# A decode step of two layers on one core: 256-key scores on four row bands for the kept heads, and a reordered group before the turn of the layers

## The chip, the cores and the metric

The kernel runs on one core of one Trainium2 chip. The time is device microseconds of one execution. The kernel before was timed three times: 513.09, 513.82 and 517.1 us, median 513.82. One further execution was profiled; its own time was 513.58 us, and the span from its first to its last instruction 511.7 us. All times of views below are microseconds from the start of that span.

## The reference

One token (S = 1, D = 640) goes through two rounds of the same pair of blocks, with the same weights and the same cache in both rounds:

```python
def _A_ref(x, k_cache, v_cache, wq, wo):
    ...
    W = min(4096, max(256, Sk // 4))
    ...
    q = (lambda x, *d: x.transpose(*d))((x @ wq).reshape(B, Sq, Hq, Dh), 0, 2, 1, 3)
    k = jnp.repeat(k_cache[:, :, Sk - W:, :], rep, axis=1)
    v = jnp.repeat(v_cache[:, :, Sk - W:, :], rep, axis=1)
    scores = jnp.einsum("bhqd,bhkd->bhqk", q, k) * (Dh ** -0.5)
    p = _softmax(scores, axis=-1)
    o = jnp.einsum("bhqk,bhkd->bhqd", p, v)
    return (lambda x, *d: x.transpose(*d))(o, 0, 2, 1, 3).reshape(B, Sq, Hq * Dh) @ wo
...
x = A_x
x = x + _A_ref(_layernorm(x, axis=-1), A_k_cache, A_v_cache, A_wq, A_wo)
x = x + _B_ref(_layernorm(x, axis=-1), B_w1, B_w2, B_w3, B_w4)
x = x + _A_ref(_layernorm(x, axis=-1), A_k_cache, A_v_cache, A_wq, A_wo)
x = x + _B_ref(_layernorm(x, axis=-1), B_w1, B_w2, B_w3, B_w4)
return x
```

There are 32 heads with Dh = 192, each with its own K and V, of which the last W = 4096 keys count. K and V of one head are 1536 KB each in bf16. `_B_ref` is a small MLP; with S = 1 its shifted first half is zero, so only w3 and w4 are used. Almost all of the work is reading: K, V, wq, wo, w3 and w4, some 214 MB.

## The kernel before

**Tiling.** A head's 4096 keys lie on 128 partitions, 32 keys in a partition. DVE turns K in place in blocks of 32x32 words (`transpose_half`, L441, two instructions a head). The scores are products with a small block of q as the weights (16 columns: four heads times four row groups) and 512 columns of turned K as the moving operand: six weight blocks times two halves of the keys, 12 products a head (L526). The two halves write different row bands of one PSUM bank, 16 rows at row 0 and 16 at row 32 of a half of the bank; the four heads of a group add up in the same rows. So the scores of a group stand on 64 partitions with 512 keys each, and the next group uses the other 64 partitions.

**Softmax.** `softmax_steps` gives seven steps: `part_max` (DVE reduction of the 64x512 scores, L552), `turn_max` (PE turns the 64 maxima into a row, pmT_ps, L557), `full_max` (DVE, L562 and L565), `spread_max` (PE copies the row back into a column nb_ps, L573; ACT takes it over, L576, and makes the exponentials, L579), `turn_p` (DVE, L585 and L587), `swap` (PE, L599, then ACT L602 and the sums l_ps, L607) and `recip` (L614, L616). Their scratch words lie in o_sb.

**Products with V.** `pv` makes 16 products a head (L649), each with two columns of PT as the weights and 384 columns of V, in four row bands of one bank, O_ps. DVE turns the result into o_sb (L656), and `o_fold` (L663, L664) reduces it. `pv` can be given a function `mid` that is called after the first eight of its 16 products.

**Order.** Heads come in eight groups of four. The first layer goes from heads 28 to 31 down to 0 to 3, the second from heads 0 to 3 up. While a group's products with V run, K of the next group is turned and its scores are made. Within an engine the instructions run in the order in which the program writes them. The group before the last (`hurry` in `attention`) makes the next group's softmax as well, so that the last group starts with its PT.

**Loads.** All loads go through SP's queue in one fixed order (`layer_stream`), into twelve cells of 1536 KB; SP waits until the cell of a load is free, and until the eighth load before it has landed. Everything behind a waiting load waits too. K of heads 0 to 7 stays in its cells, turned, from the first layer to the second (NKEEP = 8), and so do a V and a wo cell; in the second layer a kept head's cell comes free when its scores are made (`give` in `S`). At the turn of the layers few cells are left for the stream. wx_sb holds the rest of w3 and w4 that doesn't fit a cell; it is loaded once, at the end of the first layer (L221, L239, L240).

**V_bank.** Four PSUM banks hold the words of one head's V (VP) from the first layer to the second (`v_words`, L638); O_2 is a part of it that the second layer's first group already uses as a second bank for products with V.

Of the kernel before, what the change touches and what calls it, by code (L numbers as in the profile page):

```python
# [18 lines left out]
P = 128  # L19
# [40 lines left out]
def kernel(  # L60
# [454 lines left out]

    def scores(h, K, ST, hq):

        ng = NGK // NT
        Q = [Qblk[:, h // QH % 2, QAT[hq] + n * QSTEP:][:, 0:QW] for n in range(NCOL)]
        T = K.rearrange("p (j g f i t) -> p g j f i t", j=NJ4, g=NGK, f=NFB, t=2)  # L520
        for f in range(NFB):
            for t in range(2):
                n = 2 * f + t
                for i in range(NT):
                    r = ST[0] + 32 * i
                    nc.tensor.matmul(  # L526
                        ST_both[r:r + QW, :].rearrange("p (g j i) -> p g j i", g=ng, j=NJ4), lhsT=Q[n],
                        rhs=T[:, ng * i:ng * (i + 1), :, f, :, t],
                        start=(hq == 0 and n == 0), stop=(hq == QH - 1 and n == NCOL - 1))

# [2 lines left out]
    nc.vector.memset(ST_both[:], 0.0)  # L533
    turn = [0]

    def next_scores():
        turn[0] += 1
        i = turn[0] % 2 * HP
        return i, ST_both[i:i + HP, :]

    def softmax_steps(n, ST, sc, space, bank=None):

        held = {}
        halves = space.bitcast(BF16)
        at, ST_ps = ST
        S, T = slice(at, at + HP), slice(HP - at, P - at)

        def part_max():  # L550
            pm = short("pm")
            nc.vector.tensor_reduce(out=pm[S, :], in_=ST_ps, op=ALU.max, axis=AX.X)  # L552
            held["pm"] = pm

        def turn_max():
            pmT_ps = psm.tile([1, HP], F32, tag="psm")
            nc.tensor.transpose(pmT_ps[0:1, :], held["pm"][S, 0:1], ident[S, S])  # L557
            held["pmT"] = pmT_ps

        def full_max():  # L560
            ngm = space[0:1, 256:256 + 2 * QH]
            nc.vector.tensor_reduce(out=ngm[:], in_=held["pmT"][0:1, :].rearrange("o (q x m) -> o x q m", q=NT, m=NM),  # L562
                                    op=ALU.max, axis=AX.XY, negate=True)
            wide = space[0:1, 306:306 + HP]
            nc.vector.tensor_scalar(  # L565
                out=wide.rearrange("o (q x m) -> o q x m", q=NT, m=NM),
                in0=ngm[:].unsqueeze(1).unsqueeze(3).broadcast_to([1, NT, 2 * QH, NM]),
                scalar1=sc[0:1, 0:1], scalar2=None, op0=ALU.mult)
            held["w"] = wide

        def spread_max():
            nb_ps = psm.tile([P, 1], F32, tag="psm")
            nc.tensor.matmul(nb_ps[S, :], lhsT=held["w"],  # L573
                             rhs=one[0:1, :], start=True, stop=True)
            nb_sb = space[S, 289:290]
            nc.scalar.copy(nb_sb[:], nb_ps[S, :])  # L576
            Pr = halves[S, 0:SW]
            lpart = space[S, 288:289]
            nc.scalar.activation(out=Pr, in_=ST_ps, func=ACTF.Exp,  # L579
                                 bias=nb_sb[:, 0:1], scale=sc[S, 0:1], accum_out=lpart[:, 0:1])  # L580
            held["Pr"], held["l"] = Pr, lpart

        def turn_p():
            held["PrT"] = halves[T, 0:SW]
            nc.vector.transpose(held["PrT"], held["Pr"])  # L585
            lh = space[S, 280:284]
            nc.vector.tensor_scalar(out=lh[:], in0=hm[S, :], scalar1=held["l"][:, 0:1], scalar2=None, op0=ALU.mult)  # L587
            held["lh"] = lh

        def swap():  # L590
            ng = NGK // NT
            if bank is None:
                PT_ps = psm.tile([P, n, NJ4, NGK], F32, tag="psm")
            else:
                PT_ps = bank[:, 0:n * NJ4 * NGK].rearrange("p (h j g) -> p h j g", j=NJ4, g=NGK)
            src = held["PrT"].rearrange("p (g j i) -> p i j g", g=ng, j=NJ4)
            for m in range(NM):
                for q in range(NT):
                    nc.tensor.matmul(PT_ps[32 * m:32 * (m + 1), :, :, ng * q:ng * (q + 1)], lhsT=Eq[T, (HP - at) // 32 + q, :],  # L599
                                     rhs=src[:, m:QW:NM], start=True, stop=True)  # L600
# [24 lines left out]
    O_ps = O_bank[:, 0:2 * Dh]  # L625
    V_bank = psV.tile([P, 2048], F32, name="V_ps")
    O_2 = V_bank[:, 1024:1024 + 2 * Dh]
    h_ps = V_bank[:, VW:VW + NF // 2], O_bank[:, 2 * Dh:2 * Dh + NF // 2]

    def v_words(layer):  # L630
# [90 lines left out]
    def attention(layer, x_cur, rs_cur, x_new, z_new, rs_new, ss_new):  # L721
# [56 lines left out]
        for step in qa[1:]:  # L778
            step()
        qb[1]()  # L780
        ST = next_scores()
        q1 = qproj_steps(groups[1][0] // QH, xc)
        for hq, h in enumerate(groups[0]):
            for half in range(2):
# [30 lines left out]
        for gi, cur in enumerate(groups):  # L815
# [6 lines left out]
            if nxt:  # L822
                part_max, turn_max, full_max, spread_max, turn_p, swap, recip = softmax_steps(
                    len(cur), ST, sc, o_words, V_bank if layer == 1 and gi > 0 else None)
                ST_n = next_scores()
                if layer == 1 and gi == 0:

                    keep = [hh for hh in nxt if hh[1] < NKEEP]
# [23 lines left out]
                else:  # L852
# [7 lines left out]
                    turn_max()  # L860
                    full_max()
                    spread_max()
                    S(h0, 1, ST_n, 0)
                    h1 = nxt[1][1]
                    q = None
                    if gi + 2 < len(groups):
# [4 lines left out]
                    if layer == 1:  # L871
                        turn_p()
                        PT = swap()
                    if pending is not None:
                        y_ps = out_row(layer, *pending, acc, gi - 1 == rows[0]) if in_row else out_proj(layer, pending)
                    if layer == 0:
# [27 lines left out]
            for hq, h in order:  # L904
# [9 lines left out]
                if layer == 1 and gi == 0:  # L914
                    pv(layer, h, hq, PT, fold, O_2 if h == order[1][1] or h == order[3][1] else O_ps)
                    if early_k:
                        early_t(early_k)

                    def fold(h=h):
                        o_fold(h, oT, rl)  # L920

                    continue
                pv(layer, h, hq, PT, steps[3] if quick and hq == 3 else fold)
                if final:
                    if hq == 0:
# [11 lines left out]
                if quick and hq == 1:  # L937
                    S(h2, 0, ST_n, q2)
                    S(h2, 1, ST_n, q2)
                    T(h3, 0)  # L940
                elif quick and hq == 2:
                    S(h3, 0, ST_n, q3)
                    o_fold(h, oT, rl)
                    S(h3, 1, ST_n, q3)
                    steps = softmax_steps(len(cur), ST_n, sc, kl[:].bitcast(F32), V_bank)
                    for step in steps[:3]:
                        step()
                    continue
                elif hurry and hq == 1:
                    (q2, h2), (q3, h3) = nxt  # L950
                    for half in range(2):
                        T(h2, half)
                        S(h2, half, ST_n, q2)
                    T(h3, 0)
                    S(h3, 0, ST_n, q3)
                    T(h3, 1)
                elif hurry and hq == 2:
                    S(h3, 1, ST_n, q3)
                    steps = softmax_steps(len(cur), ST_n, sc, o_words)
                    steps[0]()  # L960
                    steps[1]()
                elif nxt and not (hurry and hq == 3):
                    q2, h2 = nxt.pop(0)
                    for half in range(2):
                        T(h2, half)
                        S(h2, half, ST_n, q2)
                o_fold(h, oT, rl, len(groups) - 4 > gi >= 2 * layer)
                if hurry and hq == 3:
                    for step in steps[4 if quick else 2:5]:
                        step()  # L970
                    early = steps[5](), steps[6]()
            if final or layer == 1 and gi == 0:
                fold()
# [152 lines left out]
```

## Time and profile before

| | us |
|---|---|
| three timed runs | 513.09, 513.82, 517.1 |
| profiled execution, its own time | 513.58 |
| its span, first to last instruction | 511.7 |
| mean granted TensorE clock over the span | 0.722 |

| group in the profile | count | mean ns of one |
|---|---|---|
| L441 DVE, half of a head's K turned | 112 | 1759 |
| L526 PE, scores, 512 columns | 768 | 507 |
| L649 PE, products with V, 384 columns, O_ps | 968 | 405 |
| L656 DVE, result turned | 62 | 565 |
| L552 DVE, reduction of the scores, 64x512 | 16 | 674 |
| L579 ACT, exponentials, 64x512 | 15 | 773 |
| L585 DVE, turn of P, 64x512 | 15 | 706 |

The mean of a product is its whole passage through a pipeline; several are under way at a time, so the time of a group of products is read from the timeline, not from count times mean. The queue's loads are read from SP's rows in the timeline (when a load is issued) and from the DMA share in a table of stretches (how full the 16 DMA engines are). The share is made from packets, and can stand a few hundredths above 1. The granted clock is the share of full speed that PE was given.

### The profile page before, as it was taken

The numbers are of one execution on the slowest core, as the hardware profiler recorded it, in microseconds if no ns is written. First come the engines' busy times: TensorE is split into PE (matmuls) and PEld (weight loads), VectorE is DVE, ScalarE is ACT, GpSimd is POOL, SyncE is SP. The second block draws the span as 40 slices with busy tenths as digits, with TensorE's granted clock in tenths as the row PEclk, the third lists the DMA queues.
The fourth block names the chain that finished last, engine by engine and source line by source line (L and its number), as shares of the span: only waits on it lengthen the run. The fifth ranks groups of instructions, "written<-read, shape, count | busy, mean of one in ns | idle before, by whom it ended". The sixth has DMA issues, their size and how long they took to land. (4 is left out here: it accounts for less than half of the span.)

```text
span 511.7 us, 7558 instructions
## 1 busy us (share of the span) xinstructions
PE 293.1 (57%) x3188; PEld 141.8 (28%) x3188; DVE 297.4 (58%) x492; ACT 52.1 (10%) x173; POOL 3.7 (1%) x16
## 2 busy tenths in 40 slices
PE   1145747546275463855665885848474762726585
PEld 0011313213132231422232432414231331312254
DVE  2086686557574584567633236776777475656622
ACT  1000101010010101001010111011110101001101
POOL 2000000000000000000000000000000000000000
PEclk9995685858767686585665597775869596787855
DMA  8999999999999999999999999999999999999995
GB/s 369 430 430 428 430 444 430 439 430 412 454 432 409 438 420 424 432 417 453 428 376 413 369 422 428 437 430 439 427 416 439 438 425 430 417 433 432 423 409 215
DMA packets 12005, 214.50 MB, mean 419 GB/s; under 512 B 2564, under 2 KB 3076, under 8 KB 7428
## 3 DMA queue, kind: packets, MB, share of 16 engines
q1 hardware_dynamic: 11972, 214.02, 98.2%
q8 instruction: 25, 0.41, 0.3%
q14 instruction: 8, 0.07, 0.0%
HBM read 214.01 MB, written 0.00 MB: 418 GB/s over the span
## 5 line engine op out<-in xcount | busy, mean ns | idle before, releaser
L441 DVE STREAM_TRANSPOSE cell<-cell 128x1536 uint32<-128x1536 uint32 x112 | 194.6, 1759 | 35.5 <-DMA cell<-in_A_k_cache_dram 34.9
L526 PE MATMUL ST_ps<-cell,Qblk 128*16 128x512 bf16 x768 | 151.1, 507 | 71.4 <-DVE cell L441 53.8
L649 PE MATMUL O_ps<-cell,PT 128*2 128x384 bf16 x968 | 90.3, 405 | 8.3 <-DMA cell<-in_A_v_cache_dram 7.6
L526 PEld LDWEIGHTS <-Qblk 128*16 128x16 bf16 x768 | 45.3, 105 | 145.0 <-issue 123.4
L656 DVE STREAM_TRANSPOSE o_sb<-O_ps 128x384 f32<-128x384 f32 x62 | 35.0, 565 | 45.3 <-PE O_ps L649 45.3
L649 PEld LDWEIGHTS <-PT 128*2 128x2 bf16 x1024 | 36.7, 90 | 29.4 <-issue 21.5
L486 DVE TENSOR_TENSOR o_sb<-qT_ps,words 128x24 bf16<-128x24 f32 (+1 forms) x18 | 3.2, 179 | 51.1 <-PE qT_ps L482 28.9
L557 PE MATMUL pmT_ps<-ident,words 64*1 64x64 f32 x16 | 4.0, 252 | 48.7 <-DVE words L552 48.7
L585 DVE STREAM_TRANSPOSE o_sb<-o_sb 64x512 bf16<-64x512 bf16 x15 | 10.6, 706 | 24.6 <-ACT o_sb L579 24.6
L664 ACT ACTIVATE words<-oT_ps,words 32x6 bf16<-32x6 f32 x40 | 10.3, 257 | 143.0 <-PE oT_ps L663 83.1
L663 PE MATMUL oT_ps<-o_sb,Lq 128*32 128x6 f32 x160 | 12.5, 186 | 11.8 <-DVE o_sb L656 11.3
L573 PE MATMUL nb_ps<-words,o_sb 1*64 1x1 f32 x30 | 4.9, 230 | 24.8 <-DVE o_sb L565 24.8
L663 PEld LDWEIGHTS oT_ps<-o_sb,Lq 128*32 128x32 f32 x160 | 10.9, 128 | 22.4 <-issue 15.6
L461 PE MATMUL qr_ps<-wq_sb,words 128*1 128x384 bf16 x90 | 15.8, 514 | 0.0
L557 PEld LDWEIGHTS pmT_ps<-ident,words 64*1 64x1 f32 x16 | 1.2, 76 | 51.7 <-issue 51.7
L669 ACT ACTIVATE words<-oT_ps,words 32x6 bf16<-32x6 f32 x24 | 6.2, 257 | 92.1 <-PE ST_ps L526 64.3
L472 PE MATMUL qT_ps<-words,wq_sb 128*128 128x1 bf16 x210 | 7.2, 165 | 13.0 <-DMA wq_sb<-in_A_wq_dram 12.2
L552 DVE TENSOR_REDUCE words<-ST_ps 64x1 f32<-64x512 f32 x16 | 10.8, 674 | 5.0 <-PE ST_ps L526 4.9
L695 PE MATMUL yr_ps<-cell,words 128*1 128x320 bf16 x108 | 13.4, 406 | 0.0
L576 ACT COPY o_sb<-nb_ps 64x1 f32<-64x1 f32 x15 | 2.3, 153 | 95.3 <-PE nb_ps L573 95.3
L573 PEld LDWEIGHTS nb_ps<-words,o_sb 1*64 1x64 f32 x30 | 4.0, 189 | 27.8 <-issue 26.2
L579 ACT ACTIVATE o_sb<-ST_ps,o_sb,words 64x512 bf16<-64x512 f32 x15 | 11.6, 773 | 0.5
(161 smaller groups left out, 202.7 us busy)
## 6 DMA issues: line engine op xcount, KB each, us to landing
cell<-in_A_k_cache_dram SPq DMA_DIRECT2D x56, 1536.0 KB, 27.7
cell<-in_A_v_cache_dram SPq DMA_DIRECT2D x56, 1536.0 KB, 27.7
cell<-in_A_wo_dram SPq DMA_DIRECT2D x13, 960.0 KB, 27.7
wq_sb<-in_A_wq_dram SPq DMA_DIRECT2D x5, 1536.0 KB, 13.5
cell<-in_A_v_cache_dram SPq DMA_DIRECT2D x6, 768.0 KB, 23.7
cell<-in_B_w_dram SPq DMA_DIRECT2D x1, 1536.0 KB, 12.6
cell<-in_B_w_dram SPq DMA_DIRECT2D x2, 768.0 KB, 10.3
cell<-in_A_wo_dram SPq DMA_DIRECT2D x3, 480.0 KB, 17.0
```

The source lines that it names most:

```text
L441: nc.vector.transpose(Ku, Ku)
L461: nc.tensor.matmul(qr_ps[32 * i:32 * i + 1, :], lhsT=xc[:, kc:kc + 1], rhs=wq_sb[:, kc, t0 * P + i * N:t0 * P + (i + 1) * N], start=(kc == ...
L526: nc.tensor.matmul(ST_both[r:r + QW, :].rearrange("p (g j i) -> p g j i", g=ng, j=NJ4), lhsT=Q[n], rhs=T[:, ng * i:ng * (i + 1), :, f, :, ...
L552: nc.vector.tensor_reduce(out=pm[S, :], in_=ST_ps, op=ALU.max, axis=AX.X)
L573: nc.tensor.matmul(nb_ps[S, :], lhsT=held["w"], rhs=one[0:1, :], start=True, stop=True)
L579: nc.scalar.activation(out=Pr, in_=ST_ps, func=ACTF.Exp, bias=nb_sb[:, 0:1], scale=sc[S, 0:1], accum_out=lpart[:, 0:1])
L585: nc.vector.transpose(held["PrT"], held["Pr"])
L649: nc.tensor.matmul(O_ps[r:r + 2, :], lhsT=PT[:, hq, 2 * i:2 * i + 2], rhs=v_pair(V, h, 2 * i * Dh, 2 * Dh), start=(i < 4), stop=(i >= NB - 4))
L656: nc.vector.transpose(o_sb[:], O_ps.rearrange("p (e a c) -> p e c a", e=2, c=NA))
L663: nc.tensor.matmul(oT_ps[r, :], lhsT=Lq[:], rhs=o_sb[:, e, :, e], start=(e == 0), stop=(e == 1))
L664: nc.scalar.activation(oT[r, :], oT_ps[r, :], ACTF.Copy, scale=rl[r, 0:1])
L695: nc.tensor.matmul(yr_ps[32 * i:32 * i + 1, :], lhsT=oT[:, k:k + 1], rhs=wo_t[:, k * D + i * N:k * D + (i + 1) * N], start=(k == 0), stop= ...
```

## The change

Four things are changed.

1. In the second layer the scores of groups 0 and 1 (heads 0 to 7, those whose K was kept) stand on 128 partitions with 256 keys each. `next_scores` takes the number of bands (`nt`, 4 or 2); with 4 it gives one half of the bank's columns on all partitions. `scores` then makes 24 products of 256 columns a head in four row bands, in place of 12 of 512 in two. The softmax of these two groups works on 128x256, and its `swap` has 16 products in place of 8.
2. In the second layer's group 1 the scores of the next group's first head (head 8, which is loaded) are made behind `swap`, in place of ahead of the q products (`late`).
3. In the first layer's group before the last (heads 4 to 7) a new block takes the place of the `hurry` branches. Heads 5 and 7 write O_2, heads 4 and 6 O_ps. Head 5's products follow head 4's at once, then come head 1's scores, and K of heads 2 and 3 is turned in one run. The softmax of the last group gets its words in wx_sb (`wx_sb[:, 0:6 * P]`) in place of o_sb; `turn_max` is issued ahead of head 7's products, `full_max` and `spread_max` in the middle of them.
4. O_2 is cleared at the start (one DVE memset of 128x384).

The program's instructions on each engine follow this: on PE 12 weight loads and 12 products more for each of the eight kept heads, and 8 of each more for the two swaps; one memset more on DVE, the same loads in the same order on SP. Some waits change with it: the load of the w3 rest into wx_sb waits for DVE and ACT.

```diff
     def scores(h, K, ST, hq):
 
-        ng = NGK // NT
+        at, ST_ps, nt = ST
+        ng = NGK // nt
...
-                for i in range(NT):
-                    r = ST[0] + 32 * i
+                for i in range(nt):
+                    r = 32 * i
                     nc.tensor.matmul(
-                        ST_both[r:r + QW, :].rearrange("p (g j i) -> p g j i", g=ng, j=NJ4), lhsT=Q[n],
+                        ST_ps[r:r + QW, :].rearrange("p (g j i) -> p g j i", g=ng, j=NJ4), lhsT=Q[n],
...
-    def next_scores():
+    def next_scores(nt=NT):
+
         turn[0] += 1
-        i = turn[0] % 2 * HP
-        return i, ST_both[i:i + HP, :]
+        if nt == NT:
+            i = turn[0] % 2 * HP
+            return i, ST_both[i:i + HP, :], nt
+        i = turn[0] % 2 * SW // 2
+        return 0, ST_both[:, i:i + SW // 2], nt
...
-        at, ST_ps = ST
-        S, T = slice(at, at + HP), slice(HP - at, P - at)
+        at, ST_ps, nt = ST
+        np_, w = 32 * nt, 2 * SW // nt
+        S = slice(at, at + np_)
+        T, t_at = (slice(HP - at, P - at), (HP - at) // 32) if nt == NT else (S, 0)
...
-            held["PrT"] = halves[T, 0:SW]
+            held["PrT"] = halves[T, 0:w] if nt == NT else halves[T, w:2 * w]
...
     O_2 = V_bank[:, 1024:1024 + 2 * Dh]
+    nc.vector.memset(O_2, 0.0)
...
-        ST = next_scores()
+        ST = next_scores(4 if layer == 1 else NT)
...
-                ST_n = next_scores()
+                ST_n = next_scores(4 if layer == 1 and gi == 0 else NT)
...
-                    S(h0, 1, ST_n, 0)
+                    late = layer == 1 and gi == 1
+                    if not late:
+                        S(h0, 1, ST_n, 0)
...
                     if layer == 1:
                         turn_p()
                         PT = swap()
+                    if late:
+                        S(h0, 1, ST_n, 0)
...
+                if hurry and layer == 0:
+                    if hq == 1:
+                        mid = fold
+                    elif hq == 3:
+                        steps[1]()
+                        mid = steps_23
+                    else:
+                        mid = None
+                    pv(layer, h, hq, PT, mid, O_2 if hq % 2 else O_ps)
+
+                    def fold(h=h):
+                        o_fold(h, oT, rl)
+
+                    if hq == 0:
+                        continue
+                    if hq == 1:
+                        h1 = nxt.pop(0)[1]
+                        S(h1, 1, ST_n, 1)
+                        fold()
+                        (q2, h2), (q3, h3) = nxt
+                        for hh in (h2, h3):
+                            T(hh, 0)
+                            T(hh, 1)
+                        S(h2, 1, ST_n, q2)
+                    elif hq == 2:
+                        S(h3, 1, ST_n, q3)
+                        fold()
+                        steps = softmax_steps(len(cur), ST_n, sc, wx_sb[:, 0:6 * P].bitcast(F32))
+                        steps[0]()
+
+                        def steps_23():
+                            steps[2]()
+                            steps[3]()
+                    else:
+                        fold()
+                        steps[4]()
+                        early = steps[5](), steps[6]()
+                    continue
...
-                elif hurry and hq == 1:
-                    (q2, h2), (q3, h3) = nxt
-                    for half in range(2):
-                        T(h2, half)
-                        S(h2, half, ST_n, q2)
-                    T(h3, 0)
-                    S(h3, 0, ST_n, q3)
-                    T(h3, 1)
-                elif hurry and hq == 2:
-                    S(h3, 1, ST_n, q3)
-                    steps = softmax_steps(len(cur), ST_n, sc, o_words)
-                    steps[0]()
-                    steps[1]()
...
                 if hurry and hq == 3:
-                    for step in steps[4 if quick else 2:5]:
-                        step()
+                    steps[4]()
                     early = steps[5](), steps[6]()
```

More of the change, by code (lines that the diff above doesn't have):

```diff
@@ L555, in turn_max @@
         def turn_max():
-            pmT_ps = psm.tile([1, HP], F32, tag="psm")
+            pmT_ps = psm.tile([1, np_], F32, tag="psm")
             nc.tensor.transpose(pmT_ps[0:1, :], held["pm"][S, 0:1], ident[S, S])
@@ L561, in full_max @@
             ngm = space[0:1, 256:256 + 2 * QH]
-            nc.vector.tensor_reduce(out=ngm[:], in_=held["pmT"][0:1, :].rearrange("o (q x m) -> o x q m", q=NT, m=NM),
+            nc.vector.tensor_reduce(out=ngm[:], in_=held["pmT"][0:1, :].rearrange("o (q x m) -> o x q m", q=nt, m=NM),
                                     op=ALU.max, axis=AX.XY, negate=True)
-            wide = space[0:1, 306:306 + HP]
+            wide = space[0:1, 306:306 + HP] if nt == NT else space[0:1, w // 2:w // 2 + np_]
             nc.vector.tensor_scalar(
-                out=wide.rearrange("o (q x m) -> o q x m", q=NT, m=NM),
-                in0=ngm[:].unsqueeze(1).unsqueeze(3).broadcast_to([1, NT, 2 * QH, NM]),
+                out=wide.rearrange("o (q x m) -> o q x m", q=nt, m=NM),
+                in0=ngm[:].unsqueeze(1).unsqueeze(3).broadcast_to([1, nt, 2 * QH, NM]),
                 scalar1=sc[0:1, 0:1], scalar2=None, op0=ALU.mult)
@@ L576, in spread_max @@
             nc.scalar.copy(nb_sb[:], nb_ps[S, :])
-            Pr = halves[S, 0:SW]
+            Pr = halves[S, 0:w]
             lpart = space[S, 288:289]
@@ L590, in swap @@
         def swap():
-            ng = NGK // NT
+            ng = NGK // nt
             if bank is None:
@@ L597, in swap @@
             for m in range(NM):
-                for q in range(NT):
-                    nc.tensor.matmul(PT_ps[32 * m:32 * (m + 1), :, :, ng * q:ng * (q + 1)], lhsT=Eq[T, (HP - at) // 32 + q, :],
+                for q in range(nt):
+                    nc.tensor.matmul(PT_ps[32 * m:32 * (m + 1), :, :, ng * q:ng * (q + 1)], lhsT=Eq[T, t_at + q, :],
                                      rhs=src[:, m:QW:NM], start=True, stop=True)
```

## The prediction, made before the changed kernel ran

> **What bounds the kernel now.** I read the page's busy times and DMA queue first, then a table of stretches for the DMA share, then the chain of waits, and last the timeline where the DMA share falls.
>
> ```profile
> PE 293.1 (57%) x3188; PEld 141.8 (28%) x3188; DVE 297.4 (58%) x492; ACT 52.1 (10%) x173; POOL 3.7 (1%) x16
> q1 hardware_dynamic: 11972, 214.02, 98.2%
> ```
>
> No engine passes 58% of the span, while the load queue's packets fill 98.2% of the 16 DMA engines' time. The stretches say where the rest is (columns: stretch, its length, busy time of PE, PEld, DVE, ACT and POOL, granted clock, DMA share, GB/s):
>
> ```profile
> 2.60:264.00 261.40, 139.77 (x1310) 63.65 (x1314) 157.01 (x230) 22.90 (x74) 0.96 (x4) 0.73 1.00 431
> 264.00:267.00 3.00, 3.00 (x62) 1.77 (x58) 0.92 (x4) 0.26 (x1) 0.00 (x0) 0.50 0.77 261
> 267.00:291.00 24.00, 14.84 (x254) 9.37 (x245) 8.35 (x39) 3.03 (x14) 0.00 (x0) 0.50 1.01 404
> 291.00:295.00 4.00, 4.00 (x35) 1.47 (x32) 0.43 (x3) 0.47 (x2) 0.00 (x0) 0.89 0.76 284
> 295.00:503.90 208.90, 128.10 (x1459) 62.74 (x1457) 128.59 (x201) 23.03 (x76) 0.71 (x2) 0.74 1.00 427
> 503.90:511.70 7.80, 3.10 (x90) 2.66 (x87) 2.07 (x14) 1.16 (x5) 0.00 (x0) 0.50 0.24 92
> ```
>
> From 2.6 to 503.9 us the DMA share is 1.00 or 1.01 but for two dips. Gap A (264 to 267) is 3.00 x 0.23 = 0.69 us of missing transfer, gap B (291 to 295) 4.00 x 0.24 = 0.96; together 1.65 us. That sum is what this change can win, since it touches neither the bytes, nor the start, nor the 7.8 us behind the last loads. The chain of waits agrees: its long pieces from 346.6 us on are loads, down to the last.
>
> ```profile
> 470.90 23.66 DMA cell<-in_A_v_cache_dram
> 494.57 10.29 DMA cell<-in_B_w_dram
> ```
>
> Both gaps begin because SP's next load waits for a cell that PE still reads.
>
> **Part 1: products in two banks, own words for softmax (gap A).** The group is heads 4 to 7 of the first layer, next to last in order. Before:
>
> ```profile
> 258.17 0.81 PE L649 MATMUL O_ps<-cell,PT 128*2 128x384 bf16 x13
> 260.06 0.21 DVE L562 TENSOR_REDUCE o_sb<-pmT_ps 1x8 f32<-1x64 f32 x1 [0.45 <-PE oT_ps L663]
> 260.69 0.24 PE L573 MATMUL nb_ps<-words,o_sb 1*64 1x1 f32 x2 [0.68 <-DVE o_sb L565]
> 263.70 1.45 PE L649 MATMUL O_ps<-cell,PT 128*2 128x384 bf16 x16
> 265.20 2.05 SPq L182 DMA_DIRECT2D cell<-in_A_v_cache_dram  x4
> ```
>
> The turned maxima are in pmT_ps at 258.09, but the full maximum starts at 260.06: its result goes into o_sb, which head 7's fold still reads. With its words in wx_sb it needs only pmT_ps. In the second layer the same pair is 0.30 apart (transpose 316.77, reduction 317.07), so the reduction starts at 257.88 + 0.30 = 258.2 and nb_ps, 0.63 later as before (260.06 to 260.69), is ready to run at 258.8. PE runs eight of head 7's sixteen products ahead of it (258.1 to 258.5) and eight behind. Eight cost 0.4 to 0.7 us (half of a group of 16, 0.82 at clock 1.0, 1.45 at 0.5): with nb_ps's 0.24 between them V_ps is complete by 259.8, and turned by DVE (0.58) by 260.4. The 0.70 turn of P (L585), behind it on DVE, ends at 261.1; from there to the first products it is 263.70 - 262.82 = 0.88. Head 0's products start at 262.0 in place of 263.70 and end at 263.45; SP issues at 263.5 in place of 265.20, 1.7 us earlier. Before, the share was whole again 1.3 us after that issue (266.5); now that is 264.8, where it first fell at 264.5 (in half microseconds the shares from 264.5 are 0.15, 0.58, 0.57, 0.67). Some 0.2 of 0.69 is left: gain 0.5.
>
> Head 5's products move ahead of head 1's scores, which frees head 5's cell about 1.2 us earlier (a load issued at 245.47); transfers are whole there, so nothing. K of heads 2 and 3 is turned in the same DVE places; head 6's products wait for their V (from 252.3 to 253.0), so everything up to 257.0 stays. The load at 259.02 comes at about 259.8, 0.8 later. Cover: SP issued nothing more until 265.20, yet the share held until 264.5; less that load's own 960 KB (2.3 us at 431 GB/s) and 1.3 of start, 1.9 us. The w3 rest that goes into wx_sb (issued at 268.18) now also waits for the softmax words there, free by 262.5: cover 5.7 us. The new memset of V_ps lies in DVE's idle start (its neighbour of 128x512 took 0.48): nothing.
>
> From 266.4 to 291 the work waits for loads (V at 270.73 and 276.68, w4 at 284.49 by the releasers), so the 0.5 passes on to gap B.
>
> **Part 2: 256 keys on 128 partitions (gap B).**
>
> ```profile
> 288.75 2.73 PE L526 MATMUL ST_ps<-cell,Qblk 128*16 128x512 bf16 x12 [0.27 <-DVE Qblk L510]
> 291.51 0.33 SPq L157 DMA_DIRECT2D cell<-in_A_k_cache_dram  x1
> 307.83 0.82 PE L649 MATMUL O_ps<-cell,PT 128*2 128x384 bf16 x16
> ```
>
> Head 0's twelve products end at 291.48; SP issues at 291.51 into an emptying queue. They become 24 of 256 columns in four bands: 24 x 256 / 4 = 1536 columns a band, where the twelve stream 12 x 512 / 2 = 3072. The P times V products also use four bands: 16 x 384 / 4 = 1536. So I take their time, 1.45 us at clock 0.50 and 0.82 at 1.00, for 2.73 and 1.53 now. Lower end 0.82 (full clock), upper end 24 x 2.73 / 12 = 5.46 (a product costs as much as today, however short); I take 1.45, since that row has the same columns, bands and engine, and the clock was 0.50 here. So head 0 starts at 288.75 - 0.5 and ends at 289.7; SP issues at 289.75, 1.76 earlier than before, while the data ahead of it end 0.5 earlier: 1.26 won against them. The next load, behind head 1's scores, left at 293.22; now it is 289.8 + 1.45, about 291.3, 1.4 won likewise. The dip lasted from 291.5 (0.92 in the half microsecond before, then 0.41, 0.67, 0.48) to about 294.5, a third of the transfers short on average. Its first half, 291.5 to 293.0, is the waiting for the first load (0.72 of the 0.96), and a start 1.26 earlier takes nearly all of it; of the rest, while the queue fills again, I keep all: gain 0.7.
>
> The Trainium skill speaks against this part: "TensorE: Matmul & The Clock Gate", section "Back-to-back issue gap", gives about 81 ns per product at 128 columns and 131 at 512 in a stream of weight loads and products. An estimate between them, 98 ns at 256, makes 24 products 2.35 us. The trace has 1.53 / 12 = 128 ns for 512 columns, which fits, but 0.82 / 16 = 51 ns for 384 in four bands, which doesn't.
>
> The other seven kept heads shorten by 0.6 to 1.3 us each, and so do the two softmaxes: reduction 0.69, exponential 0.77 and turn 0.70 handle half the columns. The swap has 16 products for 8 (0.44 before; at most 0.88). All of this is under a DMA share of 1.00: nothing.
>
> Moving head 8's scores behind the swap adds about 1.4 us to the cell whose K load left at 321.95; queued behind it on PE are out_proj's products and head 4's, and on SP every later load. Cover: from 291.51 to 315.13 nine loads of 1536 KB, one of 960 and one of 384 were issued, 15.5 MB, 36 us at 431 GB/s, so the queue lasts to about 328.5. That leaves 6.6 us, less 1.3 of start and the 1.2 won: nothing.
>
> **Sum.** 0.5 + 0.7 = 1.2 us. The profiled execution took 513.58 us (span 511.7 and 1.9 around it), so 512.4; the median of the three runs, 513.82, is 0.24 above it. I keep 512.4.
>
> **Rivals.**
> - A floor per weight load and product: twice as many of half the length, and head 0's scores stay at 2.73, B with them. Only A's 0.5 is won: 513.1. By the Trainium skill's estimate above, 2.35, it would be 0.4 less. For: twice the products and weight loads (PEld's mean for them is 105 ns). Against: 51 ns in four bands. Chance 0.12.
> - The gaps close but a later dip takes it back: cells come free at PE's pace between 295 and 346, and a queue that is 1.2 us ahead finds its cell taken. Then 513.6. For: SP's issues wait for PE until 346.64. Against: the reserve above. Chance 0.13.
> - Slower: products in four bands of 16 rows, not 2, cost as much each as those of 512. Head 0 takes 5.46, ends at 293.7, and SP issues 2.2 us later than before: 513.58 + 2.2 = 515.8, A's gain being eaten in the same wait. It decides from 24 x 135 ns = 3.23, where B's loss equals A's 0.5. Against: the columns above. Chance 0.07.
> - Forecast, 1.2 of 1.65 won: 0.62. The rest, 0.06, is what I don't see.
>
> **Numbers.** A measurement here tells some 1% (5.1 us) from no change. The whole missing transfer between start and tail is 1.65 us, so faster by more than that has 0.02; slower, a queue stall that I don't see, 0.05; same 0.93. Low end: the fastest run, 513.09, less 1.65 = 511.4. High end: the median without a gain, 513.8, and half a microsecond of the runs' spread: 514.4. The slower rival lies outside.
>
> **What would show it.** In the changed profile: DMA share near 1 around 264 to 267 and 290 to 294; the four V loads out near 263.6; score groups of 24 at 128x256 near 1.45 us at clock 0.5 and 0.8 at 1.0; the first K load of head 8 near 289.8; no new dip up to 346. Scores over 2.7 us, or a dip near 325, would make the prediction wrong.

## The result, and the profile after

| kernel | set of runs | runs | median us | lowest to highest |
|---|---|---|---|---|
| before | first | 8 | 513.85 | 512.78 to 517.10 |
| changed | first | 8 | 511.79 | 511.58 to 512.13 |
| before | third | 27 | 513.01 | 511.73 to 516.07 |
| changed | third | 12 | 512.20 | 511.41 to 513.52 |

The ratio of changed to before is 0.9952, with a 95% interval of 0.9934 to 0.9971, in the first set of runs, and 0.9981 (0.9968 to 0.9995) when it was measured again in the third (the second holds experiments 1 to 4). So the change makes the kernel faster by something between 0.05% and 0.7%, which is less than the 1% that the prediction took for the least that a measurement can tell. The forecast of 512.4 us is 0.6 above the first median. As a gain it was 1.2 us; the runs side by side give 2.1 in one set and 0.8 in the other, and 0.9952 times 513.82, the median that the prediction had of the kernel before, is 511.35, just below its low end of 511.4.

The profiled execution of the changed kernel took 512.13 us, its span 510.3 (before: 513.58 and 511.7). Busy times and the load queue from its page:

```profile
span 510.3 us, 7783 instructions
PE 290.5 (57%) x3300; PEld 144.4 (28%) x3300; DVE 297.1 (58%) x493; ACT 51.8 (10%) x173; POOL 3.7 (1%) x16
q8 instruction: 26, 0.43, 0.3%
```

PE has 112 products more and is 2.6 us less busy; DVE, which has the largest share, is nearly unchanged (297.1 for 297.4). The table of stretches, with the columns of the prediction (length, busy time of PE, PEld, DVE, ACT, POOL, clock, DMA share, GB/s), cut finer behind gap A:

```profile
2.60:264.00 261.40, 140.16 (x1352) 65.09 (x1353) 158.63 (x235) 23.11 (x75) 0.96 (x4) 0.75 1.00 431
264.00:267.00 3.00, 0.84 (x12) 0.37 (x15) 0.00 (x0) 0.10 (x1) 0.00 (x0) 0.50 0.85 357
267.00:281.00 14.00, 8.18 (x119) 4.80 (x112) 5.45 (x18) 1.40 (x7) 0.00 (x0) 0.50 1.01 412
281.00:284.00 3.00, 1.22 (x46) 1.14 (x44) 1.82 (x13) 1.33 (x6) 0.00 (x0) 0.50 0.95 334
284.00:290.00 6.00, 5.21 (x125) 4.05 (x126) 1.23 (x11) 0.30 (x2) 0.00 (x0) 0.50 1.02 404
290.00:295.00 5.00, 4.49 (x101) 3.00 (x90) 0.81 (x5) 0.46 (x2) 0.00 (x0) 0.75 0.95 333
295.00:502.40 207.40, 126.95 (x1477) 63.11 (x1477) 127.06 (x198) 22.66 (x76) 0.71 (x2) 0.71 1.00 429
```

In the DMA share, gap A (264 to 267) rose from 0.77 to 0.85 and gap B, taken from 290 to 295, from 0.80 to 0.95. Between them is a dip that the kernel before did not have: 281 to 284 moves 334 GB/s, where it moved 416. The two stretches of before:

```profile
281.00:284.00 3.00, 1.78 (x61) 1.70 (x61) 1.63 (x15) 1.06 (x4) 0.00 (x0) 0.50 1.11 416
290.00:295.00 5.00, 5.00 (x39) 1.73 (x36) 0.43 (x3) 0.47 (x2) 0.00 (x0) 0.82 0.80 310
```

The timeline shows what starts the loads at the three places (start, duration, engine, line, operation, operands, count, idle time and its releaser). At gap A, products in two banks, with the other words and the turned maxima between them:

```profile
256.04 0.21 PE L564 MATMUL pmT_ps<-ident,words 64*1 64x64 f32 x1 [0.87 <-DVE words L559]
256.29 0.21 DVE L569 TENSOR_REDUCE wx_sb<-pmT_ps 1x8 f32<-1x64 f32 x1 [0.40 <-PE pmT_ps L564]
256.61 0.50 PE L657 MATMUL V_ps<-cell,PT 128*2 128x384 bf16 x8 [0.36 <-DMA cell<-in_A_v_cache_dram]
257.04 0.27 PE L580 MATMUL nb_ps<-words,wx_sb 1*64 1x1 f32 x2
257.24 0.50 PE L657 MATMUL V_ps<-cell,PT 128*2 128x384 bf16 x8
260.25 1.45 PE L657 MATMUL O_ps<-cell,PT 128*2 128x384 bf16 x16
261.74 2.58 SPq L182 DMA_DIRECT2D cell<-in_A_v_cache_dram  x4
```

The full maximum (L569) starts 0.25 us behind the turn into pmT_ps, where before it waited until 260.06 for head 7's fold; SP issues the four V loads at 261.74 in place of 265.20. Part of this is the granted clock, which was 1.00 here from 250 to 258 and 0.50 to 0.54 in the profile of before; experiment 5 has the comparison at half clock. At the new dip, the last w3 products on a cell and the load that takes the cell, in the changed kernel and then in the kernel before:

```profile
280.82 0.78 PE L1059 MATMUL O_ps<-words,cell 128*128 128x1 bf16 x24
281.63 3.79 SPq L157 DMA_DIRECT2D cell<-in_A_v_cache_dram  x2
```

```profile
281.68 0.78 PE L1023 MATMUL O_ps<-words,cell 128*128 128x1 bf16 x24
282.49 3.72 SPq L157 DMA_DIRECT2D cell<-in_A_v_cache_dram  x2
```

SP issues 0.03 us behind those products in both, so it waits for PE there too. Why the queue runs empty only in the changed kernel is seen in the landings. A load is split over the 16 DMA engines and lands with 16 completions, one for each engine's part. On average over four profiled executions of each kernel, this V load leaves 0.6 us earlier (281.84 for 282.45). The load ahead of it, the last of w4, is complete on its first engine 1.8 us earlier (282.12 for 283.90), and on its last 0.6 us earlier. So the first engine is out of work 0.3 us after the V load is issued, where it was 1.45 us. And at gap B, the first two heads of layer 2:

```profile
287.94 1.46 PE L527 MATMUL ST_ps<-cell,Qblk 128*16 128x256 bf16 x24 [0.28 <-DVE Qblk L510]
289.45 0.33 SPq L157 DMA_DIRECT2D cell<-in_A_k_cache_dram  x1
289.46 1.46 PE L527 MATMUL ST_ps<-cell,Qblk 128*16 128x256 bf16 x24
290.96 0.33 SPq L182 DMA_DIRECT2D cell<-in_A_v_cache_dram  x1
```

Twenty-four products of 256 columns take 1.46 us, where twelve of 512 took 2.73.

### The profile page after: what moved, and what is told of

Same layout as the page of the kernel before. It is cut to its first block, busy times and chain, and to the rows that moved or that the text cites. A ratio compares the mean times of both kernels' runs of the same rounds, so it can differ in the third digit from the quotient of the medians.

```text
span 510.3 us, 7783 instructions
## 1 busy us (share of the span) xinstructions
PE 290.5 (57%) x3300; PEld 144.4 (28%) x3300; DVE 297.1 (58%) x493; ACT 51.8 (10%) x173; POOL 3.7 (1%) x16
## 5 line engine op out<-in xcount | busy, mean ns | idle before, releaser
L527 PE MATMUL ST_ps<-cell,Qblk 128*16 128x512 bf16 (+1 forms) x864 | 147.5, 478 | 72.0 <-DVE cell L441 56.0
L664 DVE STREAM_TRANSPOSE o_sb<-O_ps 128x384 f32<-128x384 f32 x60 | 33.8, 563 | 48.3 <-PE O_ps L657 48.3
L657 PEld LDWEIGHTS <-PT 128*2 128x2 bf16 x1024 | 38.0, 91 | 34.7 <-issue 25.4
L564 PE MATMUL pmT_ps<-ident,words 64*1 64x64 f32 (+1 forms) x16 | 4.2, 263 | 45.7 <-DVE words L559 45.7
L592 DVE STREAM_TRANSPOSE o_sb<-o_sb 64x512 bf16<-64x512 bf16 (+1 forms) x14 | 9.4, 668 | 22.3 <-ACT o_sb L586 20.7
L580 PE MATMUL nb_ps<-words,o_sb 1*64 1x1 f32 (+1 forms) x28 | 5.0, 244 | 24.3 <-DVE o_sb L572 24.3
L559 DVE TENSOR_REDUCE words<-ST_ps 64x1 f32<-64x512 f32 (+1 forms) x16 | 10.2, 640 | 3.8 <-PE ST_ps L527 3.7
L580 PEld LDWEIGHTS nb_ps<-words,o_sb 1*64 1x64 f32 (+1 forms) x28 | 4.2, 206 | 27.0 <-issue 26.0
L583 ACT COPY o_sb<-nb_ps 64x1 f32<-64x1 f32 (+1 forms) x14 | 2.2, 154 | 89.1 <-PE nb_ps L580 89.1
L472 PEld LDWEIGHTS <-wq_sb 128*128 128x128 bf16 x210 | 6.7, 101 | 15.2 <-DMA wq_sb<-in_A_wq_dram 13.0
```

The costliest lines, as they stand in the source:

```text
L472: nc.tensor.matmul(qT_ps[:, tl:tl + 1], lhsT=wq_sb[:, kc, t * P:(t + 1) * P], rhs=xc[:, kc:kc + 1], start=(kc == 0), stop=(kc == ND - 1))
L527: nc.tensor.matmul(ST_ps[r:r + QW, :].rearrange("p (g j i) -> p g j i", g=ng, j=NJ4), lhsT=Q[n], rhs=T[:, ng * i:ng * (i + 1), :, f, :, t] ...
L580: nc.tensor.matmul(nb_ps[S, :], lhsT=held["w"], rhs=one[0:1, :], start=True, stop=True)
L657: nc.tensor.matmul(O_ps[r:r + 2, :], lhsT=PT[:, hq, 2 * i:2 * i + 2], rhs=v_pair(V, h, 2 * i * Dh, 2 * Dh), start=(i < 4), stop=(i >= NB - 4))
L664: nc.vector.transpose(o_sb[:], O_ps.rearrange("p (e a c) -> p e c a", e=2, c=NA))
```

## The experiments

The theory: the gain lies at the turn of the layers alone, because the loads restart earlier at gaps A and B. The rival: shorter scores and softmaxes of the kept heads are worth something throughout. Experiments 1 to 4 are the second set, in which 25 runs of the kernel before have a median of 513.39; 5 to 7 and the first execution of 8 are the third.

**1. The reordered first-layer group alone.**

```diff
-        ST = next_scores(4 if layer == 1 else NT)
+        ST = next_scores()
-                ST_n = next_scores(4 if layer == 1 and gi == 0 else NT)
+                ST_n = next_scores()
-                    late = layer == 1 and gi == 1
+                    late = False
```

> Only the reordered group of the first layer (two banks, own words), scores of the second layer as before. Theory 1 (the gain is the transfer that was missing in the two dips): the dip at 264 to 267 closes, the one at 291 to 295 stays near 0.9 us; 0.5 us faster than before, ratio about 0.999. Theory 2 (spared PE and DVE time counts throughout): next to nothing, since this part spares none. If this part alone brings 1.5 us or more, its price was mis-sized.

Measured: 512.22 us, median of 12; ratio 0.9979 (0.9962 to 0.9996), so 1.1 us of 513.39. The stretches of its profiled execution:

```profile
264.00:267.00 3.00, 0.63 (x10) 0.24 (x11) 0.00 (x0) 0.26 (x1) 0.00 (x0) 0.50 0.90 381
281.00:284.00 3.00, 1.24 (x48) 1.16 (x45) 1.56 (x13) 1.53 (x7) 0.00 (x0) 0.50 0.93 327
290.00:295.00 5.00, 5.00 (x31) 1.59 (x29) 0.42 (x3) 0.46 (x2) 0.00 (x0) 0.66 0.90 340
```

Gap A is nearly closed, and the dip at 281 to 284 is there: it comes from this part. The queue that was refilled earlier also runs out earlier, since the next V load waits for the products on w3's cell. Gap B misses 0.5 us of transfer (5.00 x 0.10), not the 0.9 that was expected to stay.

**2. The 256-key scores alone** (with head 8's scores behind the swap): the branch of the changed order for the first layer's next to last group is taken out, and the old branches stand.

```diff
-                if hurry and layer == 0:
...
-                    continue
+                elif hurry and hq == 1:
+                    (q2, h2), (q3, h3) = nxt
...
+                    steps = softmax_steps(len(cur), ST_n, sc, o_words)
```

> Only the 256-key scores of the second layer's first two groups, with head 8's scores behind the swap; the first layer's group as before. Theory 1: the dip at 264 to 267 stays near 0.7 us, the one at 291 to 295 falls below 0.3; 0.7 us faster than before, ratio about 0.9985. Theory 2: nearly the whole gain of 2 us is here, since here is the spared time.

Measured: 511.82, median of 8; ratio 0.9971 (0.9957 to 0.9984), so 1.5 us.

```profile
264.00:267.00 3.00, 3.00 (x62) 1.69 (x54) 0.76 (x3) 0.26 (x1) 0.00 (x0) 0.50 0.76 264
281.00:284.00 3.00, 1.32 (x50) 1.24 (x47) 1.59 (x14) 1.48 (x7) 0.00 (x0) 0.50 1.07 418
290.00:295.00 5.00, 4.54 (x105) 3.15 (x98) 0.93 (x7) 0.46 (x2) 0.00 (x0) 0.78 1.00 374
```

Gap A is as before, the new dip is absent, and gap B is gone. The gain is more than the 0.7 us expected: this part alone gives about what the whole change gives. The intervals of experiments 1 and 2 overlap, so their times do not rank the two parts.

**3. The change without moving head 8's scores.**

```diff
-                    late = layer == 1 and gi == 1
+                    late = False
```

> The changed kernel with head 8's scores ahead of the q products and the swap again. Both theories: as the changed kernel, 511.8 within 0.3 us; the queue is full there.

Measured: 511.97, median of 12; ratio 0.9969 (0.9958 to 0.9979). Within the intervals of experiments 2 and 4, so the move is worth nothing that shows.

**4. 256 keys for all groups of both layers.**

```diff
-        ST = next_scores(4 if layer == 1 else NT)
+        ST = next_scores(4)
-                ST_n = next_scores(4 if layer == 1 and gi == 0 else NT)
+                ST_n = next_scores(4)
-                    late = layer == 1 and gi == 1
+                    late = False
```

> The changed kernel with 256-key scores on four bands for all groups of both layers, so some 0.6 to 1.3 us of PE and 1 us of DVE and ACT less in each of 14 more groups' heads and softmaxes. Theory 1: as the changed kernel, 511.8 within 0.3 us, since none of it lies at a dip, except what the faster last softmax saves behind the last K (the queue is full there too). Theory 2: faster again by 1 us or more.

Measured: 511.66, median of 6; ratio 0.9965 (0.9953 to 0.9977). Shorter scores in every group bring nothing that shows beyond experiments 2 and 3, where the rival asks for 1 us or more. The rival falls.

**5. The changed kernel again.**

> The changed kernel once more, as the measure for the two runs with doubled scores. Theory 1: 511.8 within 0.4 us, and a narrower spread than the kernel before has on the same chip (before: some 4 us between lowest and highest; here under 1.5), because its loads no longer hang on the granted clock at the dips. Rival (the kernel before was only unlucky in its runs): the same spread as before.

Measured: 512.20, median of 12, 511.41 to 513.52; before 513.01; ratio 0.9981 (0.9968 to 0.9995). The gain is smaller than in the first set, and the spread is 2.1 us, not the 0.6 of the first eight runs; the kernel before spreads over 4.3. The spread of under 1.5 us that was expected is missed. Its profiled execution had PE at half clock ahead of gap A, as the profile of before had, so the prediction's times can be checked here:

```profile
258.05 0.21 PE L564 MATMUL pmT_ps<-ident,words 64*1 64x64 f32 x1 [0.88 <-DVE words L559]
258.93 0.24 PE L580 MATMUL nb_ps<-words,wx_sb 1*64 1x1 f32 x2 [0.25 <-DVE wx_sb L572]
259.65 0.47 SPq L55 DMA_DIRECT2D cell<-in_A_wo_dram  x1
263.48 1.82 SPq L182 DMA_DIRECT2D cell<-in_A_v_cache_dram  x4
```

**6. Head 0's scores of layer 2 made twice**, which leaves the output as it is.

```diff
-    def scores(h, K, ST, hq):
+    def scores(h, K, ST, hq, alone=False):
...
-                        start=(hq == 0 and n == 0), stop=(hq == QH - 1 and n == NCOL - 1))
+                        start=(hq == 0 and n == 0), stop=((alone or hq == QH - 1) and n == NCOL - 1))
...
+                if (layer, hq, half) == (1, 0, 1):
+                    scores(h, Th[h, 0], ST, hq, True)
```

> The changed kernel with head 0's scores in the second layer made twice (24 more products, some 1.3 us at clock 0.5, just ahead of the cell's release at 289.45). Theory 1: the dip at 290 to 295 comes back with 0.8 to 1.2 us, and the time grows by as much. Rival (a later load takes up any delay): no change.

Measured: 511.82, median of 10; ratio 0.9974 (0.9959 to 0.9988). The doubled scores and the issue behind them:

```profile
288.57 2.74 PE L527 MATMUL ST_ps<-cell,Qblk 128*16 128x256 bf16 x48 [0.27 <-DVE Qblk L510]
291.36 0.33 SPq L157 DMA_DIRECT2D cell<-in_A_k_cache_dram  x1
292.79 0.33 SPq L182 DMA_DIRECT2D cell<-in_A_v_cache_dram  x1
298.29 0.47 SPq L55 DMA_DIRECT2D cell<-in_A_k_cache_dram  x1
```

and the stretch around them:

```profile
290.00:295.00 5.00, 5.00 (x125) 3.33 (x117) 0.61 (x4) 0.46 (x2) 0.00 (x0) 0.75 0.90 342
```

For head 0, PE's time (2.74 us) and SP's first issue (291.36) are back where the kernel before had them (2.73 and 291.51). The dip comes back in part: the share of 0.90 is 0.5 us of missing transfer, where the expectation had 0.8 to 1.2 and the first profile of before has 1.0. The other kept heads' scores stay short here, and the loads behind the first do not fall back as far. The fifth load from this issue on leaves at 298.29, against 297.17 in the changed kernel and 301.65 in the kernel before:

```profile
301.65 0.47 SPq L55 DMA_DIRECT2D cell<-in_A_k_cache_dram  x1
```

The time does not come back at all: it lies 0.4 us below experiment 5's, with intervals that overlap. So the expectation failed twice, in the size of the dip and in the time, and the next experiments look for what the time follows.

**7. The same doubling away from any dip**, at the first scores of layer 2's sixth group, with the same change to `scores`.

```diff
...
+                    if layer == 1 and gi == 4:
+                        scores(h0, Th[h0, 0], ST_n, 0, True)
```

> The changed kernel with the first scores of the second layer's sixth group made twice (12 more products of 512 columns, 1.5 to 2.7 us of PE), ahead of the same wait for a cell, where the load queue is full. Theory 1: no change, within 0.3 us. Rival: as much slower as at the dip, or more.

Measured: 512.18, median of 12; ratio 0.9974 (0.9958 to 0.9990), against 512.20 in experiment 5. PE's work under a full load queue costs nothing that shows, as the theory has it.

**8. Further profiled executions of both kernels, unchanged**: the kernel before once more, and later two more of each (b and c below).

> The kernel before once more, for another profile. Theory 1: its time less the transfer that is missing in its two dips is the same as in the first profile, within 0.4 us (513.6 less 1.5), whatever its time; the dips are of other sizes. Rival: the dips are as in the first profile and the difference lies in the transfers.

Measured: 513.36, span 511.6. Its dips are smaller than in the first profile:

```profile
264.00:267.00 3.00, 2.05 (x46) 1.41 (x46) 0.75 (x3) 0.26 (x1) 0.00 (x0) 0.50 0.81 304
290.00:295.00 5.00, 5.00 (x40) 1.67 (x35) 0.43 (x3) 0.47 (x2) 0.00 (x0) 0.77 0.89 333
```

Time less missing share is 511.9 us in the first profile (513.58 - 1.69) and 512.2 here (513.36 - 1.12). That is inside the 0.4 us that the expectation allows, so this execution leaves the theory standing. The next two do not: b has 512.8 (514.31 - 1.51, shares 0.78 and 0.83) and c 511.7 (512.83 - 1.12, shares 0.76 and 0.92). These lie 1.1 us apart, so time less missing share is not a constant of the kernel. What the time follows was worked out from the trace's records of packets and of landings, and put to the test:

> The kernel before, unchanged, one more look. Theory (the end follows the slowest DMA engine): in the ten executions so far the span ended 3.22 to 3.30 us behind the last of the 16 completions of the last w3 load, and 4.9 to 6.4 us behind their mean, so here the span is that last completion plus 3.2 to 3.3 again; the mean completion lies at 505.1 to 506.0 us, as in the two executions of this kernel so far, and the last lags it by anything from 1.7 to 3.2. Rival (the mean share sets the end): span less mean completion is the same as in the profiled executions of the same kernel to 0.3 us.

> As for the look just before: span = last completion of the last w3 load + 3.2 to 3.3 us, mean completion 505.1 to 506.0, lag between 1.7 and 3.2. The two looks differ in their spans by the difference of their lags plus that of their means; the rival has equal lags.

> The changed kernel, unchanged, one more look. Theory: mean completion of the last w3 load at 504.3 to 504.7 us (504.38 and 504.46 so far), which is the part that the change moves; the last completion lags it by 1.7 to 3.2 like the kernel before's, and the span is that plus 3.2 to 3.3. If the change's gain lay in the lag, the mean would be at 505 or later.

> As for the look just before: mean completion 504.3 to 504.7 us, lag 1.7 to 3.2, span = last + 3.2 to 3.3.

The load that these texts mean is the kernel's last, of w4; they call it w3's by mistake. For the four executions of each kernel (us; "lag" is last less mean completion):

```
                 span   mean of 16   last   lag   span - last
before, first    511.7    505.95    508.46  2.51     3.24
before, exp. 8   511.6    505.18    508.32  3.14     3.28
before, b        512.5    506.71    509.28  2.57     3.22
before, c        511.1    506.10    507.81  1.71     3.29
changed, first   510.3    504.46    507.08  2.62     3.22
changed, exp. 5  509.6    504.38    506.38  2.00     3.22
changed, b       510.5    504.98    507.23  2.25     3.27
changed, c       509.6    504.30    506.37  2.07     3.23
```

The span follows the last completion (3.22 to 3.29 in all eight), as expected; the lag lies in the range given, and the rival, which has it equal within a kernel, falls (1.71 to 3.14). The ranges given for the mean were too narrow: three of the four new executions lie above them. On average the spans differ by 511.73 - 510.00 = 1.73 us, of which the mean completion has 505.99 - 504.53 = 1.46 and the lag 2.48 - 2.24 = 0.25. The waits on the last w3 load, with the two spans furthest apart, read alike:

```profile
505.73 0.48 PE L1023 MATMUL V_ps<-words,cell 128*128 128x1 bf16 x12 [0.89 <-DMA cell<-in_B_w_dram]
```

```profile
502.98 0.48 PE L1059 MATMUL V_ps<-words,cell 128*128 128x1 bf16 x12 [1.92 <-DMA cell<-in_B_w_dram]
```

The first is execution b of the kernel before (span 512.5), the second execution c of the changed one (509.6): 6.8 and 6.6 us remain behind them.

Where the 1.46 us arise is read from the bytes that have arrived by a given moment, worked out from the packets. MB, as means of the four executions of each kernel, with experiments 1 and 2 (one execution each); the last three columns are MB ahead of the kernel before, divided by 0.431 MB per us:

```
  by us   before  changed   exp. 1   exp. 2 | changed  exp. 1  exp. 2 ahead, us
   264    112.60   112.60   112.62   112.65 |   0.0     0.1     0.1
   267    113.56   113.84   113.90   113.59 |   0.6     0.8     0.1
   281    119.29   119.70   119.76   119.37 |   0.9     1.1     0.2
   284    120.47   120.67   120.67   120.59 |   0.4     0.5     0.3
   294    124.08   124.41   124.26   124.40 |   0.8     0.4     0.7
   300    126.34   126.89   126.56   126.92 |   1.3     0.5     1.3
   310    130.54   131.17   130.74   131.21 |   1.5     0.5     1.6
   330    139.15   139.79   139.34   139.83 |   1.5     0.4     1.6
```

All of the gain arises between 264 and 310 us, and nothing is lost or won behind that. Gap A's part is 0.9 us ahead by 281, and half of it goes in the new dip. At gap B the kernel before falls behind until 300 or later, not only until 294: in the six microseconds behind the dip it moves 2.26 MB, the changed kernel 2.48, and the DMA share is no lower in that stretch than elsewhere (1.01 in the first profile of before, from 294 to 300). The packets themselves are slower: those of 48 KB that start in this stretch take 1.8 to 3.1 us in that profile, most of them over 2.0, where 1.82 is usual in both kernels and nearly all take that in the first profile of the changed one. Experiment 2 is as far ahead by 310 as the whole change.

One execution can't carry a small difference here. By 310 the four of the kernel before lie between 0.7 us behind their mean and 0.8 ahead of it, and the four of the changed kernel between 1.0 and 1.7 ahead of that mean. Experiment 1's 0.5 lies inside the first range, experiment 2's 1.6 outside. Between 284 and 310 alone, experiment 1 gains nothing, the changed kernel 1.0 on average and experiment 2 1.3: what is won at gap B comes with the 256-key scores.

## Why the prediction was wrong, and where it was right

**What failed**: two steps. "So the 0.5 passes on to gap B" had the overlap wrong: half of the lead that gap A gives is lost in a new dip at 281 to 284. And the term of gap B, "gain 0.7", was too small: the bytes say 1.0 to 1.3 us, because it was read off the missing DMA share. The bound of 1.65 us came from the same shares, and the low end of the range was the fastest of three runs less this bound.

**What bounds the kernel, and where the gain lies**: right. Loads set the end, the gain arises between 264 and 310 us, around the two gaps, and experiments 4 and 7 show no worth of PE's time elsewhere in either direction.

**Gap A's order**: right, to 0.2 us where the clock is the same. Experiment 5 has the other words' products at 258.93 (forecast 258.8), the next wo load at 259.65 (259.8) and the V loads at 263.48 (263.5). "Everything up to 257.0 stays" holds only there: in the first profile of the changed kernel PE ran at full clock from 250 to 258, the maxima were turned at 256.04, and the loads left at 261.74.

**"So the 0.5 passes on to gap B"**: wrong in kind. The forecast took the stretch from 266.4 to 291 for one where the work waits for loads only; the V load at 282.49 waits for PE's products on w3's cell. A queue that is refilled earlier runs empty there, and experiment 1 shows the dip alone with this part. The changed kernel is 0.9 us ahead by 281 and 0.4 by 284. That this is near the forecast 0.5 is luck: twice as much was won at gap A, and half of it was lost again.

**The scores' cost**: right. 1.46 us at half clock (1.45 forecast) and 0.87 to 0.89 at full clock (0.82), so a product in four bands took 61 and 36 ns. The estimate of 2.35 us from the Trainium skill's "TensorE: Matmul & The Clock Gate", section "Back-to-back issue gap", is not borne out, and neither are the rivals that need dear short products. The same page's section "Part 3: Packing small matmuls", by which products on different tiles of the array run side by side, fits the row, and was the one to weigh. SP issued at 289.45 (289.75) and 290.96 (291.3).

**"Gain 0.7" at gap B**: the mechanism is right and the size is too small. It was taken from the missing DMA share between 291.5 and 294.5. The bytes say 1.0 us for the changed kernel and 1.3 in experiment 2, from 284 to 310. Some 0.7 us of that comes behind 294, where the share reads 1.00 again and the transfers of the kernel before are still slow. For the same reason "1.65 is what this change can win" was no bound: a share counts a packet as busy however slowly it moves.

**The other kept heads at nothing**: not shown, and experiment 6 speaks against it. Experiments 3 and 4 leave these heads as they are. In experiment 6 the first load is as late as in the kernel before, and by 294 its lead over that kernel is 0.1 us, as it was at 284. By 310 it is 0.8. Over that stretch it wins as much as the changed kernel does, and what it still has over the kernel before is the shorter scores and softmaxes of the other seven heads, and the loads that leave earlier behind them. This is one execution, and no run here lengthens these heads' scores alone.

**Head 8's scores and the later softmaxes at nothing**: nothing shows (experiments 3 and 4), with no dip up to 346; the stretch from 295 to 502.4 has a share of 1.00.

**The sum**: 0.5 + 0.7 = 1.2 against 1.46 in the mean landing and 1.73 in the spans of four executions each. That the sum is so near is luck in part, since gap A's own gain was put too low and the loss behind it at nothing. The range missed what single executions of the kernel before differ by: it allowed half a microsecond, and its 60 runs in the three sets lie between 511.73 and 517.10, so the fastest of three (513.09) was no floor to subtract from. That is also why one measurement gave 2.1 us and another 0.8. Which of the two is nearer stays open.

**Experiment 6's time** stays open too, but there is less to explain than it seems. Its loads arrive 0.7 us later than the changed kernel's (139.48 MB by 330 us against 139.79), and 0.35 of that is missing by 284, ahead of the doubled scores: gap A had half clock throughout, and the V loads left at 264.25. What the doubling cost in this execution is some 0.35 us, and its last completion lags the mean by 1.77 us, where the four executions of the changed kernel have 2.24. Ten runs with this spread can't tell such a difference.

Nothing run here clearly beats the changed kernel. Experiments 2, 3 and 4 equal it within their intervals, so the reordered group has shown no worth of its own beside the 256-key scores.

## What to carry to other kernels

Where loads bound a kernel, price a dip by the bytes that have arrived behind it, not by the missing share of busy time: the share reads 1.00 again while the transfers still run below their rate. A queue that is refilled earlier also empties earlier, so look up the next issue that waits for an engine, and follow the lead only up to there. And take several executions of the kernel before: one profile's gaps, and one execution's time, differ by as much as such a change is worth.

## What the runs showed of the hardware

The sixteen parts of one load drift apart during a run, and the latest sets the end. In the eight executions above, first and last completion of a load lie 0.5 to 1.0 us apart at 40 us, 1.9 to 2.4 at 100, 3.4 to 4.0 at 256, and 3.5 to 4.7 at the end. For the second load that is issued at gap B (landing near 298) it was 1.25 to 1.4 in three executions of the kernel before and 1.7 to 2.0 in the changed kernel. So the late parts can catch up while a queue is short of work. They need not: in the first profile of before, whose dip at gap B is the deepest, it was 3.45 there. Whether a dip gives some of its cost back in this way was not tried by itself.

In the first profile of before, the drift grows in three large steps of some 1.6 us, at 49, 239 and 419 us, and packets of 16 KB on the instruction queue, about 1.0 us each, start at 46.5, 236.5 and 415.3. The Trainium skill ("Runtime: NRT & Kernel Launch", section "Instruction fetch mechanics") says that code is fetched in such blocks by a DMA queue, at a cost that is mostly hidden. The trace agrees with the size, and the changed kernel's page above counts 26 of them. Only three of the 25 in the first profile of before fall on a step, and experiment 4, with 32, is not slower; that the fetches cause the steps is a guess, and no run here took them away.
